# Nine unread products instead of sixteen ahead of unit 0's transposes, and alpha transposed behind group 0: a fused attention and MLP kernel on one Trainium2 core

## The chip, the cores and the metric

The kernel runs on one core of one Trainium2 chip. The metric is the device time in microseconds (us) of one execution. The engines of the core are PE (TensorE, matrix products), DVE (VectorE), ACT (ScalarE), POOL (GpSimd) and SP (SyncE, which here only issues transfers). A transfer (DMA) runs on 16 DMA engines, whichever queue issued it.

## The reference

A causal linear attention with a decay per head feeds a two-layer MLP with a leaky activation. Cut to what matters (B = 4 batches, H = 8 heads, S = 768 positions, D = 64; the MLP is 512 to 2048 to 512 wide):

```python
for b in range(nb):                        # blocks of 64 positions
    intra = einsum('bhic,bhjc->bhij', qb, kb) * Dmask       # lam ** (i - j), lower half
    intra = einsum('bhij,bhjd->bhid', intra, vb)
    inter = einsum('bhid,bhde->bhie', qb * lam_pow, kv_state)
    out[:, :, sl] = intra + inter
    kv_state = lam_block * kv_state + einsum('bhsd,bhse->bhde', kb * rev_pow, vb)
x = out.transpose(0, 2, 1, 3).reshape(B * S, H * D)
h = x @ w_in
g = maximum(h, 0) + alpha * minimum(h, 0)
result = g @ w_out
```

## The kernel before

**Units and chunks.** The sequence is cut into three windows of 256 positions (two blocks of 128 each). A *unit* is one window of one batch and four of its heads (`hh`), 24 units in all; four units make a *chunk* `c` of two batches, 512 rows of the MLP. For a unit the kernel casts keys, queries and values to 16 bits (`cast`, L247), multiplies the keys by their decay (`key_decayed`, L260, tile `kdec`), transposes keys and queries on PE through a PSUM bank (`transposed`, L303, tile `tpx`, four products of 128x128, then a copy into `qkT`), and multiplies the transposed queries by their decay (`decayed`, L321, tile `qdT`).

**Groups.** `cluster(old, new)` (L336) puts the products of two units together on PE: for the old unit the products with the carried state (L351) and with the masked scores (L380), for the new one the scores (L368, banks `s0` and `s1`) and the new state products (L395). They share the bank `acc`. Behind it stand the mask multiplication (DVE, L406), the copy of the finished attention output to `xT` (L234), and the state updates (ACT L426 and L427, DVE L430). What this text calls group 0 is `cluster(None, 0)`, group 1 is `cluster(0, 1)`.

**MLP.** `up(c, f)` (L449) multiplies `xT` by one 128-wide slice of `w_in` and applies the activation on ACT (L462) and DVE (L471, which needs `oma` = 1 - alpha); `down` (L478) multiplies by `w_out` and stores.

**Constants and the first microseconds.** `lam` and `alpha` come by two ACT-issued transfers (L61, L64). DVE zeroes the state tiles `RD` (`zero_states`, L115), POOL builds the identity `ident`. PE transposes a tile of `lam` (L170, `lam_ps`); its logarithm starts everything that decays. `slopes()` (L221) transposes alpha on PE (`at_ps`, L223) and has DVE make `oma` (L224).

**Unread products.** `fill(n, bank)` (L130) issues n products of 128x512 of the identity with itself (L134, tile `unread`), whose results nobody reads. They occupy PE in between. A bank has one tile (`op`, `tk`) or two in turn (`h`); whoever allocates a bank waits until its last tile has been read.

**What sets the order.** Nothing is reordered: each engine does its instructions in the order in which the program lists them, and waits on semaphores. Up to chunk 1 the order is a hand-written list (L554 to L771); from chunk 2 on, `weave` (L543) mixes attention steps and MLP steps. SP issues all loads of keys, queries and values in list order. `gate(i, which)` (L109) is a tiny transfer on SP that reads a slice of a weight, so that the loads behind it on SP wait until that slice has landed; POOL issues the loads of the weight slices (`load_win`, L95; `load_wout`, L101) in its own order between its casts. The start of the list around the change:

```python
    mask_logs(1)
    mask_logs(2)
    slopes()
    decay_mask(1)
...
    cast(0, "k16", "V")
    fill(16, "h")
    transposed(0, 1, "V", "tk")
    cast(1, "k16", "A")
    fill(3, "h")
    transposed(1, 1, "V", "h")
    load(0, 0, "q", 1)
    cast(1, "q16", "A")
    transposed(0, 0, "V", "op")
```

Of the kernel before, what the change touches and what calls it, by code (L numbers as in the profile page):

```python
# [11 lines left out]
def kernel(  # L12
# [16 lines left out]
    nc = tc.nc  # L29
# [42 lines left out]
    RD = {  # L72
        (b, hh): const.tile([128, 2, 2, 2, D], fp16, name=f"RD{b}_{hh}")
        for b in range(B)
        for hh in range(2)
    }
# [18 lines left out]
    def load_win(i):  # L95
        nc.gpsimd.dma_start(
            out=w_in_sb[:, :, ts(i, 512)],
            in_=moe_w_in[:, ts(i, 512)].rearrange("(g p) f -> p g f", p=128),
        )
# [14 lines left out]

    def zero_states(batches):  # L115
        for b in batches:
            for hh in range(2):
                nc.vector.memset(RD[b, hh], 0.0)

    zero_states((0, 1))  # L120
    ident = const.tile([128, 128], fp16, name="ident")
    make_identity(nc, ident)
    ident32 = const.tile([NF, NF], fp32, name="ident32")
# [2 lines left out]
    def bank_of(bank, name, dtype=fp32):  # L126
        pool = h_ps_pool if bank == "h" else ps
        return pool.tile([128, CH], dtype, tag=bank, name=name)

    def fill(n, bank="h"):  # L130

        t = bank_of(bank, "unread").rearrange("p (a j) -> p a j", a=4)
        for _ in range(n):
            nc.tensor.matmul(  # L134
                t, lhsT=ident, rhs=ident.unsqueeze(1).to_broadcast([128, 4, 128]), start=True, stop=True
            )

    lam_ps = h_ps_pool.tile([128, CH], fp32, tag="h", name="lam_ps")
    fill(2)

# [40 lines left out]
    def mask_logs(hp):  # L183

        for hl in range(2):
            h = 2 * hp + hl
            nc.vector.scalar_tensor_tensor(
                out=dmask[:, hl, hp],
                in0=rel_f,
                scalar=loglam[:, h : h + 1],  # L190
                in1=drop,
                op0=ALU.mult,
                op1=ALU.add,
            )

    def decay_mask(hp):
        nc.scalar.activation(dmask[:, :, hp], dmask[:, :, hp], AF.Exp)
# [23 lines left out]
    def slopes():  # L221
        at = h_ps_pool.tile([128, CH], fp32, tag="h", name="at_ps")
        nc.tensor.transpose(at[:, 0:NF], alpha_sb, ident32)  # L223
        nc.vector.tensor_scalar(  # L224
            out=oma, in0=at[:, 0:NF], scalar1=-1.0, scalar2=1.0, op0=ALU.mult, op1=ALU.add
        )
# [5 lines left out]
    def copy_on(eng, out, in_):  # L232
        if eng == "A":
            nc.scalar.activation(out, in_, AF.Copy)  # L234
        elif eng == "V":
            nc.vector.tensor_copy(out=out, in_=in_)
        else:
            nc.gpsimd.tensor_copy(out=out, in_=in_)  # L238
# [8 lines left out]
    def cast(n, name, eng):  # L247
        t = T.setdefault(n, {})
        if name == "v16":
            t[name] = half_pool.tile([128, 2, 4, D], fp16, tag=name, name=name)  # L250
            copy_on(eng, t[name], raw_of(n)[name])
            return
        if "qk16" not in t:
            t["qk16"] = half_pool.tile([128, 2, 2, 4, D], fp16, tag="qk16", name="qk16")
        copy_on(eng, t["qk16"][:, int(name == "k16")], raw_of(n)[name])
# [47 lines left out]
    def transposed(n, x, eng, bank):  # L303

        c, bi, hh = units[n]
        t = T.setdefault(n, {})
        if "qkT" not in t:
            t["qkT"] = qkt_pool.tile([128, 2, 2, 2, L], fp16, tag="qkT", name="qkT")
        tp = bank_of(bank, "tpx", fp16).rearrange("p (e h j) -> p e h j", e=2, h=2)
        for e in range(2):  # L310
            for hp in range(2):
                nc.tensor.transpose(  # L312
                    tp[:, e, hp, :],
                    t["qk16"][:, x, e, ds(2 * hp, 2)].rearrange("p l d -> p (l d)"),
                    ident,
                )
        copy_on(eng, t["qkT"][:, x], tp)
        if x == 0:
            t["qps"] = tp
# [233 lines left out]

    mask_logs(1)  # L554
    mask_logs(2)
    slopes()
    decay_mask(1)
    mask_logs(0)
    load(0, 0, "k", 0)
# [11 lines left out]
    cast(0, "v16", "A")  # L571
    decay_mask(3)
    cast(0, "k16", "V")
    fill(16, "h")
    transposed(0, 1, "V", "tk")
    cast(1, "k16", "A")
    fill(3, "h")
    transposed(1, 1, "V", "h")
    load(0, 0, "q", 1)
    cast(1, "q16", "A")  # L580
# [10 lines left out]
    decay_mask(0)  # L591
    fill(3, "tk")
    cluster(None, 0)
    transposed(1, 0, "V", "h")
    load_win(0)
    cast(2, "q16", "A")
    fill(5, "h")
    transposed(2, 0, "V", "op")
    load(0, 1, "q", 1)
    cast(2, "k16", "A")  # L600
# [33 lines left out]
    up(0, 5, 0, "h")  # L634
    up(0, 5, 1, "op")
    zero_states((2, 3))
    up(0, 3, None, "tk")
    up(0, 0, 1, "h")
# [175 lines left out]
```

## Time and profile before

| what | value |
|---|---|
| time, median of 3 runs (lowest to highest) | 221.18 us (220.04 to 221.42) |
| the profiled execution, its own time | 221.5 us |
| its span, first to last instruction | 219.5 us |
| mean granted PE clock | 1.000 |
| bytes moved by transfers | 33.90 MB, mean 154 GB/s |

The profile is of one execution. Its page gives busy times by engine, the span in forty slices of 5.49 us, the transfers, the chain of work that ended last, and the costliest groups; the trace behind it gives single instructions. Times in it count from the start of the span. The 2.0 us between the execution's time and its span lie outside the span.

### The profile page before, as it was taken

How to read it: one execution, taken by the hardware profiler on the slowest of the kernel's cores; microseconds unless marked ns; L12 is line 12 of the kernel's file. 1: busy time of each engine (PE TensorE's matmuls, PEld its weight loads, DVE VectorE, ACT ScalarE, POOL GpSimd, SP SyncE). 2: the span in 40 equal slices, each digit the busy share in tenths (PEclk: the TensorE clock that was granted, in tenths of full speed). 3: DMA queues.
4: the chain of work that ended last, by engine and by line, in shares of the span. 5: the costliest groups of instructions: out<-in, count | busy, mean ns of one | idle time of the engine just before them, and what ended most of it. 6: DMA issues, size and time to landing. Idle time of an engine off the chain costs nothing.

```text
span 219.5 us, 5216 instructions
## 1 busy us (share of the span) xinstructions
PE 209.1 (95%) x2079; PEld 106.9 (49%) x2079; DVE 131.8 (60%) x263; ACT 115.4 (53%) x223; POOL 89.6 (41%) x161
## 2 busy tenths in 40 slices
PE   4998899999996999999999999999999999999994
PEld 1455545554453544555545545544545444444453
DVE  7399788965696974866856555646546444444000
ACT  6747678955762565365465446445444434444121
POOL 3553056802577583597693583485331000000000
PEclk9999999999999999999999999999999999999999
DMA  6999997999989999689757877341211011100212
GB/s 168 296 235 169 245 262 193 190 197 302 238 249 122 314 284 178 185 222 218 191 118 198 217 177 196 82 99 49 51 48 48 3 48 49 48 39 12 96 48 96
DMA packets 62335, 33.90 MB, mean 154 GB/s; under 512 B 18135, under 2 KB 59367, under 8 KB 62311
## 3 DMA queue, kind: packets, MB, share of 16 engines
q1 hardware_dynamic: 58038, 29.37, 52.8%
q0 software_dynamic: 4224, 4.19, 12.1%
q8 instruction: 16, 0.26, 0.5%
q14 instruction: 9, 0.07, 0.1%
q10 hardware_dynamic: 48, 0.01, 0.0%
HBM read 27.27 MB, written 6.29 MB: 153 GB/s over the span
## 4 chain that ended last, share of the span: by engine, by line
PE 88%; ACT 4%; DMA 4%; DVE 2%; issue 1%; ACTq 0%; DVEq 0%
PE h_ps L454 37%; PE o_ps L484 30%; PE o_ps L507 6%; PE unread L134 4%; PE s L368 3%; DMA qkT<-qk 3%; PE acc L380 2%; PE acc L351 2%; PE acc L395 1%; PE tpx L312 1%; DMA alpha_sb<-in_moe_alpha_dram 1%; ACT xT L234 1%; ACT m L462 1%; ACT RD L426 1%; DVE R L430 1%
## 5 line engine op out<-in xcount | busy, mean ns | idle before, releaser
L471 DVE SCALAR_TENSOR_TENSOR g<-m,oma,h_ps 128x512 f16<-128x512 f32 (+1 forms) x100 | 71.5, 724 | 60.5 <-ACT m L462 59.5
L454 PE MATMUL h_ps<-xT,w_in_sb 128*128 128x512 f16 (+1 forms) x400 | 95.7, 371 | 0.3 <-ACT qkT L234 0.3
L462 ACT ACTIVATE m<-h_ps 128x512 f32<-128x512 f32 (+1 forms) x100 | 57.5, 580 | 63.2 <-PE h_ps L454 61.6
L484 PE MATMUL o_ps<-w_out_sb,g 128*128 128x512 f16 x320 | 81.1, 379 | 0.0
L454 PEld LDWEIGHTS <-w_in_sb 128*128 128x128 f16 x400 | 38.1, 98 | 42.1 <-issue 0.9
L484 PEld LDWEIGHTS <-g 128*128 128x128 f16 x320 | 30.3, 98 | 35.2
L444 POOL COPY RD<-R 64x128 f16<-64x128 f16 x64 | 18.5, 288 | 37.4 <-DVE R L430 35.5
L406 DVE TENSOR_TENSOR sm<-s,dmask 128x512 f16<-128x512 f32 x48 | 30.8, 683 | 3.7 <-PE s L368 3.4
L326 POOL TENSOR_TENSOR qdT<-qkT,qdecay 128x512 f16<-128x512 f16 (+1 forms) x20 | 21.4, 1071 | 11.4 <-DMA qkT<-qk 4.8
L264 POOL TENSOR_TENSOR kdec<-kraw,kdecay 128x512 f16<-128x512 f32 x21 | 21.9, 1046 | 5.1 <-DMA kraw<-in_k_dram 5.0
L497 ACT ACTIVATE o_sb<-o_ps 128x512 f32<-128x512 f32 (+1 forms) x25 | 14.5, 580 | 17.4 <-PE o_ps L507 11.1
L234 ACT ACTIVATE xT<-acc 128x512 f16<-128x512 f32 x21 | 12.5, 597 | 14.6 <-PE acc L395 11.9
L238 POOL CAST qk<-kraw 128x512 f16<-128x512 f32 x17 | 10.5, 618 | 21.7 <-DMA kraw<-in_k_dram 10.8
L430 DVE SCALAR_TENSOR_TENSOR R<-R,rdecay,acc 128x64 f16<-128x64 f16 x64 | 14.2, 274 | 1.7 <-ACT R L427 1.7
L134 PE MATMUL unread<-ident 128*128 128x512 f16 x45 | 13.8, 444 | 1.4 <-POOL ident masks.py:199 1.4
L507 PE MATMUL o_ps<-w_out_sb,g 128*128 128x512 f16 (+1 forms) x80 | 14.0, 337 | 0.0
L368 PE MATMUL s<-qkT 64*64 64x128 f16 x384 | 10.0, 222 | 1.7 <-DMA qkT<-qk 1.7
L234 ACT ACTIVATE qk<-qraw 128x512 f16<-128x512 f32 x18 | 11.2, 623 | 0.3 <-DMA qraw<-in_q_dram 0.3
L507 PEld LDWEIGHTS <-g 128*128 128x128 f16 x80 | 7.8, 98 | 6.2
L351 PEld LDWEIGHTS <-RD 128*128 128x128 f16 x80 | 6.1, 98 | 7.9 <-ACT m L462 1.1
L351 PE MATMUL acc<-qdT,RD 128*128 128x128 f16 x80 | 8.5, 219 | 1.4 <-ACT m L462 0.6
L238 POOL CAST v<-vraw 128x512 f16<-128x512 f32 x15 | 9.1, 608 | 1.6 <-PE h_ps L454 1.6
(54 smaller groups left out, 108.5 us busy)
## 6 DMA issues: line engine op xcount, KB each, us to landing
out_dram<-o_sb SPq DMA_DIRECT2D x23, 256.0 KB, 2.0
kraw<-in_k_dram SPq DMA_DIRECT2D x10, 512.0 KB, 5.5
qraw<-in_q_dram SPq DMA_DIRECT2D x10, 512.0 KB, 5.7
vraw<-in_v_dram SPq DMA_DIRECT2D x10, 512.0 KB, 5.7
w_in_sb<-in_moe_w_in_dram POOLq DMA_DIRECT2D x4, 512.0 KB, 7.7
w_out_sb<-in_moe_w_out_dram POOLq DMA_DIRECT2D x4, 512.0 KB, 7.2
kraw<-in_k_dram SPq DMA_DIRECT2D x4, 256.0 KB, 5.2
qraw<-in_q_dram SPq DMA_DIRECT2D x4, 256.0 KB, 5.3
```

The source lines that it names most:

```text
L134: nc.tensor.matmul(t, lhsT=ident, rhs=ident.unsqueeze(1).to_broadcast([128, 4, 128]), start=True, stop=True)
L234: nc.scalar.activation(out, in_, AF.Copy)
L238: nc.gpsimd.tensor_copy(out=out, in_=in_)
L264: engine(eng).tensor_tensor(out=kdec, in0=kr, in1=kdecay[:, ds(4 * hh, 4), :].rearrange("p h e -> p e h").unsqueeze(3).to_broadcast([128, ...
L326: engine(eng).tensor_tensor(out=qdT[:, :, :, p], in0=(t["qps"] if eng == "P" else t["qkT"][:, 0])[:, :, :, p], in1=qdecay[:, hh, :, :, p], ...
L351: nc.tensor.matmul(ot[a][:, hp, :].rearrange("p (e j) -> p e j", e=2), lhsT=RD[bb, ho][:, a, hp].rearrange("p h d -> p (h d)"), rhs=to["qd ...
L406: nc.vector.tensor_tensor(out=sm, in0=s[hl], in1=mask_of(hl, hh), op=ALU.mult)
L454: nc.tensor.matmul(h_ps[:, 0:n] if bi is None else h_ps[:, 0:n].rearrange("p (e j) -> p e j", e=2), lhsT=w_in_sb[:, gi, ts(f, 128)], rhs=x ...
L462: nc.scalar.activation(m[:, 0:n], h_ps[:, 0:n], AF.Relu, scale=-1.0)
L471: nc.vector.scalar_tensor_tensor(out=g, in0=mv, scalar=oma[:, f : f + 1], in1=hv, op0=ALU.mult, op1=ALU.add)
L484: nc.tensor.matmul(o_ps, lhsT=lhs(c, f, t), rhs=w_out_sb[:, f, :], start=(f == 0), stop=(f == NF - 1),)
L507: nc.tensor.matmul(o_ps[:, 0:n], lhsT=lhs(c, f, t), rhs=w_out_sb[:, f, ts(x, n)], start=(f == 0), stop=(f == NF - 1),)
```

## The change

Four things are edited. The two unread products ahead of the transpose of `lam` become four, and they read the zeroed state tile `RD[1, 1]` in place of the identity; that tile is now zeroed first. `slopes()` moves from the mask logarithms to the place behind group 0. Sixteen unread products ahead of unit 0's key transposes become nine. The three behind those transposes and the five behind unit 1's query transposes take the bank `tk` and not `h`. In all PE issues five products fewer; DVE does `oma` behind the state update of group 0, and `zero_states` counts down where it counted up. ACT, POOL and SP keep their instructions and their order.

```diff
     def zero_states(batches):
         for b in batches:
-            for hh in range(2):
+            for hh in (1, 0):
                 nc.vector.memset(RD[b, hh], 0.0)
 
-    zero_states((0, 1))
+    zero_states((1, 0))
...
-    def fill(n, bank="h"):
-
-        t = bank_of(bank, "unread").rearrange("p (a j) -> p a j", a=4)
+    def fill(n, bank="h", zeros=None):
+
+        t = bank_of(bank, "unread")
         for _ in range(n):
+            if zeros is not None:
+                nc.tensor.matmul(t, lhsT=zeros[:, 0:128], rhs=zeros, start=True, stop=True)
+                continue
             nc.tensor.matmul(
-                t, lhsT=ident, rhs=ident.unsqueeze(1).to_broadcast([128, 4, 128]), start=True, stop=True
+                t.rearrange("p (a j) -> p a j", a=4),
+                lhsT=ident,
+                rhs=ident.unsqueeze(1).to_broadcast([128, 4, 128]),
+                start=True,
+                stop=True,
             )
 
     lam_ps = h_ps_pool.tile([128, CH], fp32, tag="h", name="lam_ps")
-    fill(2)
+    fill(4, "h", RD[1, 1].rearrange("p a e h d -> p (a e h d)"))
...
     mask_logs(1)
     mask_logs(2)
-    slopes()
     decay_mask(1)
...
     cast(0, "k16", "V")
-    fill(16, "h")
+    fill(9, "h")
     transposed(0, 1, "V", "tk")
     cast(1, "k16", "A")
-    fill(3, "h")
+    fill(3, "tk")
     transposed(1, 1, "V", "h")
...
     fill(3, "tk")
     cluster(None, 0)
+    slopes()
     transposed(1, 0, "V", "h")
     load_win(0)
     cast(2, "q16", "A")
-    fill(5, "h")
+    fill(5, "tk")
     transposed(2, 0, "V", "op")
```

## The prediction

> **What bounds the kernel now.** I read the page first: span, engine shares, the forty slices of the DMA engines, the costliest group.
>
> ```profile
> span 219.5 us, 5216 instructions
> PE 209.1 (95%) x2079; PEld 106.9 (49%) x2079; DVE 131.8 (60%) x263; ACT 115.4 (53%) x223; POOL 89.6 (41%) x161
> DMA  6999997999989999689757877341211011100212
> L454 PE MATMUL h_ps<-xT,w_in_sb 128*128 128x512 f16 (+1 forms) x400 | 95.7, 371 | 0.3 <-ACT qkT L234 0.3
> ```
>
> PE is busy 95% of the span, and the 400 up-projection products waited 0.3 us in all (last column). From the first of them on, PE is an almost gapless queue in a written order: work that reaches it earlier ends the kernel earlier, one for one, unless a transfer takes the lead back. The DMA engines are nearly full for the first 16 slices, so that can happen. The change lies in the first two slices. There the chain of waits (start, length, what) reads:
>
> ```profile
> 4.14 0.26 PE at_ps L223
> 4.40 5.60 PE unread L134 x16
> 10.00 0.22 PE tpx L312 x4
> 10.22 0.65 PE unread L134 x3
> ```
>
> Alpha's transpose, which waited for alpha's load, starts at 4.14, and behind it stand sixteen unread products whose results nobody reads. They hold back unit 0's key transposes, although the timeline (start, length, engine, line; in brackets the idle time before and what ended it) shows the keys cast long before, and DVE idle 3.09 us for them:
>
> ```profile
> 6.75 0.42 DVE L236 CAST qk<-kraw 128x512 f16<-128x512 f32 x1
> 9.83 0.39 PE L312 MATMUL tpx<-ident,qk 128*128 128x128 f16 x4
> 10.26 0.42 DVE L236 COPY qkT<-tpx 128x512 f16<-128x512 f16 x1 [3.09 <-PE tpx L312]
> 7.65 0.61 ACT L234 ACTIVATE qk<-kraw 128x512 f16<-128x512 f32 x1
> 10.70 0.61 PE L312 MATMUL tpx<-ident,qk 128*128 128x128 f16 x8
> 11.94 0.42 PE L368 MATMUL s<-qkT 64*64 64x128 f16 x16
> 4.33 3.17 PE L134 MATMUL unread<-ident 128*128 128x512 f16 x7
> ```
>
> The last row gives PE's first pace: seven products in 3.17 us, the last one lasting about 0.61, so six steps of 0.427 us. The chain's three products from 10.22 take 0.65, or 0.217 each. The sixteen of the chain took 5.60, that is ten at the first pace and six at the second: PE halves its step near 8.6 us, though the granted clock of a window quoted below (third number from the end) reads 1.00. Both paces are used below.
>
> **The change part by part.** *Zeros.* The four products on zeros need only the first memset, not ident. The four memsets begin at 0.86 and take 1.09, so the first ends near 1.15; four steps of 0.427 end at 2.9. The lambda transpose behind them started at 2.85, so it moves by at most 0.1, and what follows it on ACT and DVE too. Their cover is the wait for lambda; without it they would cost 1.7. Against that 0.1, DVE no longer has oma between the mask logarithms, where it takes about 0.1 of its queue:
>
> ```profile
> 0.86 1.09 DVE L118 MEMSET RD<- 128x256 uint32 x4 [0.86 <-PEq L798]
> 2.85 0.27 PE L170 MATMUL lam_ps<-ident,lamc 8*128 8x8 f32 x1 [0.45 <-DVE lamc L163]
> 5.03 0.16 DVE L224 TENSOR_SCALAR oma<-at_ps 128x16 f32<-128x16 f32 x1
> ```
>
> So the key cast still ends at 6.75 + 0.42 = 7.17.
>
> *Nine for sixteen, alpha away.* PE goes on at about 3.2 without alpha. Nine products end at 3.2 + 9 x 0.427 = 7.04 even if all go at the slow pace. The key transposes then wait for the cast alone and start at 7.2 instead of 9.83: 2.6 us ahead.
>
> *The next three products move to bank tk.* That bank holds the key transposes until DVE has copied them, so here is a new wait. By the rows above the copy starts 0.43 after the transposes and takes 0.42: 7.63 to 8.05. The three products run from 8.08 and take 0.65, and the eight transposes behind them start at 8.73 instead of 10.70. Unit 1's keys, cast by ACT at 7.65 + 0.61 = 8.26, are there. The wait takes 0.6 of the 2.6; 1.97 is left. Copies follow at 9.16 to 9.92 and the scores of group 0 at 9.97 instead of 11.94.
>
> *What else group 0 needs.* These rows decide whether the lead goes on:
>
> ```profile
> 7.73 2.06 POOL L264 TENSOR_TENSOR kdec<-kraw,kdecay 128x512 f16<-128x512 f32 x2 [5.01 <-DMA kraw<-in_k_dram]
> 9.73 0.61 POOL L238 CAST v<-vraw 128x512 f16<-128x512 f32 x1
> 11.98 1.06 POOL L264 TENSOR_TENSOR kdec<-kraw,kdecay 128x512 f16<-128x512 f32 x1
> 11.99 1.34 DVE L326 TENSOR_TENSOR qdT<-qkT,qdecay 128x256 f16<-128x256 f16 x1
> 45.14 0.42 DVE L326 TENSOR_TENSOR qdT<-qkT,qdecay 128x256 f16<-128x256 f16 x1
> 13.32 0.62 ACT L234 ACTIVATE qk<-qraw 128x512 f16<-128x512 f32 x1
> 14.00 0.40 PE L312 MATMUL tpx<-ident,qk 128*128 128x128 f16 x4
> 5.89 0.69 SPq L87 DMA_DIRECT2D qraw<-in_q_dram  x1
> qraw<-in_q_dram SPq DMA_DIRECT2D x1, 256.0 KB, 5.3
> ```
>
> POOL's decayed keys depend on a load and stay put; unit 0's end at 7.73 + 2.06 = 9.79, and its state products want them at 12.16 - 1.97 = 10.19, so 0.4 of slack is left of 2.4. DVE's qdT took 1.34 instead of 0.42 because it stood beside a POOL tensor operation (11.98 to 13.04) and ended 0.29 after it. In the new order it falls at 9.95, beside POOL's cast that ends at 10.34, and ends near 10.63: that is 2.7 earlier than 13.33, so DVE does not lose the lead. The Trainium skill ("SBUF — State Buffer", Who interferes with whom) calls the port pair of VectorE and GpSimd an exclusive lock: the loser waits for the winner's whole instruction. The two qdT rows agree, and by that rule the delay would be the same 0.3 to 0.4.
>
> *Alpha behind group 0.* Its transpose is 0.26 by the chain's row, and oma 0.16 on DVE; nobody needs oma before the first up-projection, so it costs PE some 0.2. The transposes of unit 1's queries start near 10.65, five products on tk (which waits for no reader) fill to 11.95, and unit 2's query transposes need ACT's cast, which was the 13.32 row: 13.32 + 0.62 - 1.97 = 11.97. Its data came at 5.89 + 5.3 = 11.2 (the last two rows are that load's issue and its time to landing), just ahead of 11.35, so 0.15 of slack. They start at 12.0 instead of 14.00: 2.0. Group 1's scores stood on a DVE copy, and DVE is 2.3 to 2.7 ahead, so PE leaves group 1 with a lead of 2.0 to 2.3.
>
> *Where the lead meets loads.* The first up-projection stood at 22.32 and needs the first w_in slice, which landed at 10.28 + 6.7 = 17.0: it can come at 20. The next loads hang on a gate, a small transfer that waits for the second w_in slice. I hold that slice where it was: POOL issues the first pair from 10.28 on, behind work that does not move.
>
> ```profile
> 10.28 1.69 POOL L96 DMA_DIRECT2D w_in_sb<-in_moe_w_in_dram  x2
> w_in_sb<-in_moe_w_in_dram POOLq DMA_DIRECT2D x1, 512.0 KB, 6.7
> 22.32 1.05 PE L454 MATMUL h_ps<-xT,w_in_sb 128*128 128x256 f16 x8
> 29.21 0.61 POOL L238 CAST qk<-kraw 128x512 f16<-128x512 f32 x1 [10.84 <-DMA kraw<-in_k_dram]
> 32.16 0.39 PE L312 MATMUL tpx<-ident,qk 128*128 128x128 f16 x4
> 30.95 0.61 POOL L238 CAST qk<-qraw 128x512 f16<-128x512 f32 x1
> 33.80 0.72 PE L312 MATMUL tpx<-ident,qk 128*128 128x128 f16 x8 [0.28 <-DVE g L471]
> 22.60 3.75 SPq L87 DMA_DIRECT2D vraw<-in_v_dram  x1
> vraw<-in_v_dram SPq DMA_DIRECT2D x1, 512.0 KB, 10.1
> 34.77 0.62 ACT L234 ACTIVATE v<-vraw 128x512 f16<-128x512 f32 x1
> ```
>
> Unit 4's keys are cast at 29.82 at the earliest and PE wanted them at 32.16: room for 2.3. Its queries are cast at 31.56, wanted at 33.80: room for 2.2. Its values land at 22.60 + 10.1 = 32.7 and were cast at 34.77: room for 2.1. These three cap the lead at about 2.1. Later transfers are released by POOL's w_out issues, which follow PE, so they move with it; the page's seventh DMA slice (32.9 to 38.4) stands at 7 tenths, room for those slices to start earlier.
>
> The sum: 2.63 (transposes), minus 0.66 (tk wait and order), plus 0 to 0.3 (DVE), capped at 2.1. I take 2.1. The profiled execution took 221.5 us, 0.3 above the median of 221.18; 221.5 - 2.1 = 219.4. Ends of the unknown prices: a gate that opens 1 us later leaves a lead of 1.1; one that opens some 0.6 earlier, because the microsecond in which the DMA engines were busy only 0.67 (the row below, next to last number) is filled, lifts the cap to 2.7.
>
> ```profile
> 18.00:19.00 1.00, 1.00 (x36) 0.67 (x34) 1.00 (x3) 0.99 (x3) 0.37 (x1) 1.00 0.67 82
> ```
>
> **The rivals.** *A: the transfers keep the lead.* The engines are full, the gated loads stay where they are or come later because the second pair of w_in slices is now issued 2.3 earlier among them. For it: the three rooms above are all near 2.1, so every microsecond that a load slips is lost at once. Against it: those slices stand behind the first pair on one queue. With slips of 1 to 2 the lead is 0 to 1.1 and the time 220.4 to 221.5.
>
> *B: PE falls to its slow pace* (the slower side). With seven unread products fewer, PE idles up to 1.1 us ahead of 7.2 (if its pace doubles at 5, nine products end near 6.1) and again 0.5 behind the key transposes. If that keeps or brings back the 0.427 step, every microsecond of fast work costs another. It decides where 2.1 us of such work has run slow, that is if the slow pace lasts to about 12.3; if it lasts to 16.7, the loss is 2.1 more, and the time 223.6. Against it: PE once stood still 1.68 us, and the eight products behind it kept the short step ((1.90 - 0.38) / 7 = 0.217, the last lasting 0.38):
>
> ```profile
> 69.83 0.42 PE L368 MATMUL s<-qkT 64*64 64x128 f16 x16 [1.68 <-DMA qkT<-qk]
> 70.53 1.90 PE L454 MATMUL h_ps<-xT,w_in_sb 128*128 128x512 f16 x8
> ```
>
> The Trainium skill ("TensorE: Matmul & The Clock Gate", Part 1 and Part 4) states that the array runs at half rate until a free-running window of some 3.4 us was busy, falls back after an idle one, and that transposes do not count as busy. By that rule the idle here would not be long enough for a fall, while a window of mostly transposes and waits could be. The two rows agree on the first half; no row here shows the second.
>
> *C: more than forecast.* The gated loads come earlier as above: lead 2.3 to 2.7, time 218.8 to 219.2.
>
> **How the numbers follow.** Forecast (218.9 to 220.0): 0.52. A: 0.24. B: 0.09, most of it between no change and 223.6. C: 0.15. The range for 8 in 10 runs from C's lower part to the top of A: 218.4 to 221.5. About 1%, or 2.2 us, is what a measurement of this kernel can tell from no change. Against 221.18 that is 218.97, just under my 219.4: all but a little of C (0.13) and some two fifths of the forecast's own band (0.22) would count as faster, 0.35; slower is the far part of B, 0.05; the rest, 0.60, is the same.
>
> **What would show it.** The key transposes start at 7.2, right behind DVE's cast; the eight that follow at 8.7, after a wait of PE for the copy on tk; group 0's scores at 10.0; the first up-projection near 20.1; unit 4's transposes at 29.9 and 31.6. If the first holds and the last two stay at 32 to 34, A is right; steps of 0.427 behind 9 us show B; scores later than 10.5 mean a wait that I have not priced.

## The result and the profile after

The median fell from 221.18 us to 219.92 us (17 runs each, 220.04 to 222.53 and 218.70 to 222.11). The ratio is 0.9943, with a 95% interval of 0.9921 to 0.9964: 1.26 us faster. The interval excludes no change, though the gain is less than the 1% that the prediction took as the least that can be told from none. The forecast was 219.4 us, a lead of 2.1 us against the profiled execution that it started from. The direction, the range and the place in the kernel were right; two fifths of the forecast lead did not come.

The page of the profile after, its span, PE's share and the group of the up-projections:

```profile
span 218.7 us, 5205 instructions
PE 208.0 (95%) x2074; PEld 106.4 (49%) x2074; DVE 131.4 (60%) x263; ACT 115.3 (53%) x223; POOL 89.6 (41%) x161
L461 PE MATMUL h_ps<-xT,w_in_sb 128*128 128x512 f16 (+1 forms) x400 | 95.7, 371 | 0.3 <-ACT qkT L241 0.3
```

PE is as full as before and does the same 95.7 us of up-projections; its busy time is 1.1 us shorter, with five products fewer. The kernel is still one PE queue, 0.8 us shorter in this pair of profiles (219.5 and 218.7; the profiled execution after took 220.56 us, against 221.5 before).

The timeline of PE after, over the front of the kernel (start, length, what; in brackets PE's idle time before and what ended it):

```profile
1.19 1.89 PE L135 MATMUL unread<-RD 128*128 128x512 f16 x4 [1.19 <-DVE RD L118]
3.01 0.27 PE L177 MATMUL lam_ps<-ident,lamc 8*128 8x8 f32 x1
3.21 3.43 PE L137 MATMUL unread<-ident 128*128 128x512 f16 x9
7.30 0.40 PE L319 MATMUL tpx<-ident,qk 128*128 128x128 f16 x4 [0.66 <-DVE qk L243]
8.21 0.81 PE L137 MATMUL unread<-ident 128*128 128x512 f16 x3 [0.52 <-DVE qkT L243]
8.86 0.61 PE L319 MATMUL tpx<-ident,qk 128*128 128x128 f16 x8
10.09 0.42 PE L375 MATMUL s<-qkT 64*64 64x128 f16 x16
13.28 0.42 PE L375 MATMUL s<-qkT 64*64 64x128 f16 x16
20.29 1.05 PE L461 MATMUL h_ps<-xT,w_in_sb 128*128 128x256 f16 x8
```

The steps that the prediction named stand where it put them (its figure in brackets): key transposes 7.30 (7.2), the eight behind them 8.86 (8.7), scores of group 0 at 10.09 (10.0), first up-projection 20.29 (20.1, before 22.32). The bracket at 7.30 says that the keys' cast on DVE ends the wait, no longer the unread products; the one at 8.21 is the new wait for bank `tk`. The lead at the first up-projection is 2.03 us. The timeline after, where unit 4 needs its transfers:

```profile
19.47 0.74 SPq L113 DMA_DIRECT2D gates<-w_in_sb  x1
26.87 0.61 POOL L245 CAST qk<-kraw 128x512 f16<-128x512 f32 x1 [10.53 <-DMA kraw<-in_k_dram]
30.13 0.39 PE L319 MATMUL tpx<-ident,qk 128*128 128x128 f16 x4
31.77 0.72 PE L319 MATMUL tpx<-ident,qk 128*128 128x128 f16 x8 [0.28 <-DVE g L478]
```

Here the forecast had its cap. It did not bind: in this pair unit 4's keys are cast 2.3 us earlier than before (29.21), PE arrives 2.03 earlier (32.16 and 33.80 before), and the transposes do not wait for a load. The lead is lost later, in chunk 2. The first score groups of that chunk, before and then after:

```profile
59.28 0.42 PE L368 MATMUL s<-qkT 64*64 64x128 f16 x16
64.40 0.42 PE L368 MATMUL s<-qkT 64*64 64x128 f16 x16
```

```profile
57.25 0.42 PE L375 MATMUL s<-qkT 64*64 64x128 f16 x16
62.65 0.28 PE L358 MATMUL acc<-qdT,RD 128*128 128x128 f16 x2 [0.32 <-POOL RD L451]
63.35 0.42 PE L375 MATMUL s<-qkT 64*64 64x128 f16 x16 [0.42 <-DMA qkT<-qk]
68.98 0.42 PE L375 MATMUL s<-qkT 64*64 64x128 f16 x16 [1.83 <-DMA qkT<-qk]
```

At 57.25 the lead is still 2.03. At 63.35 it is 1.05. Of this loss 0.42 is a wait of PE for the DMA transpose of unit 10, and 0.32 a wait for a state tile that POOL copies (`RD`); the kernel before had neither. At 68.98, unit 11's scores (before 69.83, with a wait of 1.68), it is 0.85, and so it stays to the end.

### The profile page after: what moved, and what is told of

Read it like the earlier page. It is cut to its first block, busy times and chain, and to the rows that moved or that the text cites. A ratio compares the mean times of both kernels' runs of the same rounds, so it can differ in the third digit from the quotient of the medians.

```text
span 218.7 us, 5205 instructions
## 1 busy us (share of the span) xinstructions
PE 208.0 (95%) x2074; PEld 106.4 (49%) x2074; DVE 131.4 (60%) x263; ACT 115.3 (53%) x223; POOL 89.6 (41%) x161
## 3 DMA queue, kind: packets, MB, share of 16 engines
q0 software_dynamic: 4224, 4.19, 11.9%
## 4 chain that ended last, share of the span: by engine, by line
PE 87%; ACT 4%; DVE 4%; DMA 3%; issue 1%; SPq 0%; ACTq 0%
PE h_ps L461 37%; PE o_ps L491 30%; PE o_ps L514 6%; PE s L375 3%; DMA qkT<-qk 3%; PE acc L387 2%; PE acc L358 2%; PE tpx L319 2%; PE acc L402 1%; DVE dmask L194 1%; PE unread L137 1%; ACT m L469 1%; PE unread L135 1%; ACT xT L241 1%; ACT RD L433 1%
## 5 line engine op out<-in xcount | busy, mean ns | idle before, releaser
L461 PE MATMUL h_ps<-xT,w_in_sb 128*128 128x512 f16 (+1 forms) x400 | 95.7, 371 | 0.3 <-ACT qkT L241 0.3
L137 PE MATMUL unread<-ident 128*128 128x512 f16 x36 | 10.6, 423 | 0.5 <-DVE qkT L243 0.5
```

What stands on the lines that cost most here:

```text
L461: nc.tensor.matmul(h_ps[:, 0:n] if bi is None else h_ps[:, 0:n].rearrange("p (e j) -> p e j", e=2), lhsT=w_in_sb[:, gi, ts(f, 128)], rhs=x ...
```

## The experiments

Two theories followed from this pair. Theory 1: the front gives 2 us, and chunk 2 takes a part of it back, since the query load of units 10 and 11 is issued by SP behind unit 8's DMA transpose and lands too late for a PE that is early. Theory 2, its rival: the pair is not typical, the front gives less than 2 us in most executions, and chunk 2 costs nothing new. In what follows "front" is the start of the first up-projection, and "rest" is the span minus that. The medians of the kernel before in the three sets were 221.34, 221.30 and 221.42 us.

**1. The loads of units 10 and 11 ahead of unit 8's transpose, after and before.** The same edit on both kernels:

```
+    load(2, 1, "q", None)
+    load(2, 1, "v", None)
     transposes(8, "D", False)
...
     key_decayed(11, "G")
-    load(2, 1, "q", None)
-    load(2, 1, "v", None)
```

> The changed kernel, with the loads of unit 10's and 11's queries and values (batch 1 of chunk 2) issued on SP ahead of unit 8's transpose instead of behind it. Theory 1: PE's lead of 2.0 us is whole until 62 us, and 1.2 of it is lost there because that load stands on SP behind a transpose that waits for a cast. Then unit 10's query cast follows POOL's decayed keys near 58.2 (59.6 in the changed kernel), PE no longer waits for unit 10's transpose at 63, and the end comes 1.0 to 1.2 us earlier than in the changed kernel: ratio to before 0.989 to 0.990. Theory 2, the lead is lost to the DMA engines themselves, which are full: the transposes land as late as now and the ratio stays at 0.994.

> The kernel before, with only the same two loads issued ahead of unit 8's transpose. Theory 1: in the kernel before PE is 2.0 us later, reaches unit 10's scores just as its transpose lands, and has no lead to lose, so the ratio is 0.998 to 1.001. Theory 3, the place of the loads costs time whatever PE's lead is: the gain is the same 1 us as on the changed kernel, ratio 0.995.

Measured: 1.0012 (0.9984 to 1.0040) on the kernel after and 1.0102 (1.0074 to 1.0130) on the one before. The remedy cost about as much in both, 0.7% and 1.0% against the unedited kernels. The timeline of the edited kernel after shows why, in SP's queue and on PE:

```profile
54.48 6.36 SPq L289 DMA_TRANSPOSE qkT<-qk  x2
60.63 0.64 PE L375 MATMUL s<-qkT 64*64 64x128 f16 x16 [3.21 <-DMA qkT<-qk]
```

Unit 8's transpose, now issued at 54.48 behind two loads, released PE only at 60.63, after 3.21 us of waiting (3.31 in the edited kernel before). In the kernel after, it was issued at 52.63 and the group stood at 57.25 without a wait. The wait also cost more than itself. The page of the edited kernel after has the granted clock of forty slices, and the twelfth, from 60.7 us, stands at 0.7; below it are the sixteen up-projection products behind the group, in this kernel and then in the kernel after:

```profile
PEclk9999999999979999999999999999999999999999
61.42 4.78 PE L461 MATMUL h_ps<-xT,w_in_sb 128*128 128x512 f16 x16
```

```profile
57.73 3.63 PE L461 MATMUL h_ps<-xT,w_in_sb 128*128 128x512 f16 x16
```

From 60.6 to 63.5 the granted clock was 0.50, and the products took 1.15 us longer. In the edited kernel before it was 0.50 from 62.9 to 66.1, and the same products took 5.31. The eight executions of the edited kernel after with a mean clock of 0.992 or less took 222.07 us or more, the four with 1.000 at most 220.99. So the order of that queue matters, but none of the expected ratios came true: PE no longer waited for units 10 and 11, the edit had moved the wait to unit 8, where it also slowed PE, and so it tells nothing on how much the first wait costs.

**2. Sixteen unread products again, the rest as after.**

```
-    fill(9, "h")
+    fill(16, "h")
```

> The changed kernel with sixteen unread products again in front of unit 0's key transposes, all else as changed. From 3.2 us on, with the pace doubling at 6.0 as in the changed kernel's trace, sixteen end at 8.1, so the key transposes start at 8.1 instead of 7.3 and the lead at group 0 is 1.2 instead of 2.0. Theory 1, a lead over 0.85 is lost at 62 us anyway: the ratio to before stays at 0.994 to 0.995, and PE does not wait at 63. Rival, every microsecond at the front is worth its share at the end: ratio 0.997 to 0.998. If nine instead of sixteen were the whole gain, the ratio would be 1.000.

Measured: 0.9960 (0.9934 to 0.9987), between the two expectations. The front stood at 20.80, half a microsecond behind the kernel after. PE was free for the key transposes at 8.05 instead of 7.30, yet most of the gain remained: with PE busy from 1.19 on and no wait for alpha, sixteen products end well ahead of the 9.83 of the profile before.

**3. Alpha's transpose back in the front, nine products as after.**

```
     mask_logs(2)
+    slopes()
...
     cluster(None, 0)
-    slopes()
```

> The changed kernel with alpha's transpose back among the mask logarithms, in front of the nine products. PE then waits for alpha until 4.1, nine products at the slow pace end near 8.2, the key transposes start near 8.2 and the lead at group 0 is 1.1. Theory 1: ratio to before 0.994 to 0.995. Rival, every microsecond at the front is worth its share at the end: 0.997 to 0.998.

Measured: 0.9953 (0.9928 to 0.9978), front 20.47. PE waited 0.83 for alpha's load and the key transposes started at 7.66. Its profile is the shortest of all, 216.8 us, and PE waited little in chunk 2. The timeline of its second and third score group there:

```profile
62.55 0.42 PE L375 MATMUL s<-qkT 64*64 64x128 f16 x16
67.16 0.42 PE L375 MATMUL s<-qkT 64*64 64x128 f16 x16 [0.83 <-DMA qkT<-qk]
```

Against the profile before this is a lead of 1.85 at the front and at 62.55 alike, with no wait. With the program of chunk 2 unaltered, the loss that theory 1 took as given is absent here: it is not there in every execution.

**4. Units 9 and 10 exchanged in chunk 2 (order 8, 9, 11, 10), after and before.** The second group, then unit 9's, takes its queries from the load that unit 8 already had. The edit exchanges the two numbers in `key_decayed`, the casts of queries and values, `transposes`, `decayed` and `cluster`:

```
-    cast(10, "q16", "G")
-    transposes(10, "D", False)
+    cast(9, "q16", "G")
+    transposes(9, "D", False)
...
-    cluster(8, 10, "V")
+    cluster(8, 9, "V")
```

> The changed kernel with units 9 and 10 exchanged in the order of chunk 2 (8, 9, 11, 10 instead of 8, 10, 11, 9) from the decayed keys on, so that the unit behind 8 needs the queries that landed at 52 and not those that land at 59.6. Theory 1, the lead is lost to the late load of unit 10's queries: the second transpose of the chunk is issued near 58.8 instead of 60.3, PE does not wait at 63, and the end is 0.8 to 1.2 us earlier than in the changed kernel, ratio to before 0.988 to 0.991. Theory 2, the loss is in the DMA engines, where the transposes stand behind the loads: it lands near 62.3 anyway and the ratio is 0.993 to 0.995.

> The kernel before with the same exchange of units 9 and 10. Theory 1: PE comes 2.0 us later there and hardly waits for the second transpose, so the exchange gains at most 0.4 us: ratio 0.998 to 1.001, and the changed kernel with it is 1.8 to 2.0 us faster than this one. Rival, the exchange helps whatever the lead is: as much as on the changed kernel.

Measured: 0.9903 (0.9867 to 0.9938), 219.28 us, on the kernel after, the best version of all; 0.9988 (0.9956 to 1.0019) on the kernel before. In the first, the second group stood at 62.18 without a wait. The medians of the two edited kernels lie 1.77 us apart, more than the 1.26 of the unedited ones. That agrees with theory 1, but the interval overlaps that of the kernel after (0.9921 to 0.9964), so the exchange is not proved to be worth anything.

**5. Unit 9's query cast and transposes ahead of unit 10's decay, after and before.**

```
+    cast(9, "q16", "G")
+    transposes(9, "D", False)
     decayed(10, "G")
     cast(10, "v16", "A")
-    cast(9, "q16", "G")
-    transposes(9, "D", False)
     cluster(8, 10, "V")
```

> The changed kernel with unit 9's query cast and its transpose put ahead of unit 10's qdT on POOL (by one instruction), because that qdT waits for PE. The last transpose of the chunk is then released by the transpose of unit 11 in front of it on SP, near 64.6 instead of 65.6; PE's wait of 1.8 us at 67 falls to about 0.8. If that wait takes part of the lead: ratio to before 0.989 to 0.991. If the transpose lands as late as before because the DMA engines or the transpose in front of it set the time: 0.994.

> The kernel before with the same move of unit 9's query cast. Its wait at 68 was 1.7 us and would fall to 0.7: ratio 0.995 to 0.996 if POOL's order set it, 1.000 if the DMA engines did. The difference to the changed kernel with the same move tells what the lead is worth when that wait is short: 2.0 us by the theory that the lead is lost in this place, 1.3 if it is not.

Measured: 0.9937 (0.9912 to 0.9961) and 1.0018 (0.9989 to 1.0047): no difference to either unedited kernel. PE still waited 1.43 and 1.03 us at the third group. That group reads unit 11's transpose, and the edit moves unit 9's, which stands behind it on SP, so it could not shorten this wait directly. The edited kernel before also waited 0.81 at the second group, unit 10's, although its front was late (21.30).

The four profiles with the front of before (the kernel before and its three edits, which all lie behind 50 us) now speak on theory 2. In the timelines of the edits of 1, 4 and 5 in turn, the sixteen unread products and the first up-projection:

```profile
4.29 5.54 PE L134 MATMUL unread<-ident 128*128 128x512 f16 x16
21.73 1.05 PE L454 MATMUL h_ps<-xT,w_in_sb 128*128 128x256 f16 x8
```

```profile
4.28 5.32 PE L134 MATMUL unread<-ident 128*128 128x512 f16 x16
21.49 1.05 PE L454 MATMUL h_ps<-xT,w_in_sb 128*128 128x256 f16 x8
```

```profile
4.29 5.11 PE L134 MATMUL unread<-ident 128*128 128x512 f16 x16
21.30 1.05 PE L454 MATMUL h_ps<-xT,w_in_sb 128*128 128x256 f16 x8
```

The profile before, on which the forecast rests, has 5.66 and 22.32: the latest of the four. How long the sixteen products take depends on how long PE stays at its first pace. With fifteen steps of 0.427 or 0.217 us and a last product of 0.38, the lengths 5.66, 5.54, 5.32 and 5.11 mean 9.6, 9.1, 8.0 and 7.0 slow steps, so the pace doubled at 8.5, 8.2, 7.7 and 7.3 us. The four fronts average 21.71. The four profiles with the front of after (the kernel after and its edits of 1, 4 and 5) stand at 20.29, 20.38, 20.03 and 20.49, on average 20.30; there the key transposes start at 7.30 in each, whatever the pace was. So the front is worth 1.41 us on average, as far as four profiles of each can tell, not 2.03.

**6. All nine unread products away.**

```
-    fill(9, "h")
```

> The changed kernel without the nine unread products: PE stands still from the lambda transpose at 3.3 to the key cast at 7.25. The products are there to double PE's pace, which in the traces so far came at 6.0 with them (four zeros and nine) and at 7.3 to 8.5 in the kernel before. If the pace needs PE busy (theory), it is still 0.427 us a step at 8.2, the three and three products in front of group 0 take 1.3 each and not 0.65, group 0's scores start at 11.4 to 12.0 instead of 10.09 and the ratio to before is 0.999 to 1.003. If the pace comes with time alone (rival), the scores start at 10.1 and the ratio is 0.994.

Measured: 1.0006 (0.9983 to 1.0029), so the whole gain is gone. Its timeline of PE, and below it the row of the windows view for 7.3 to 11.9 us (third number from the end: granted clock):

```profile
7.30 0.61 PE L319 MATMUL tpx<-ident,qk 128*128 128x128 f16 x4 [4.02 <-DVE qk L243]
8.42 1.44 PE L137 MATMUL unread<-ident 128*128 128x512 f16 x3 [0.52 <-DVE qkT L243]
22.04 1.05 PE L461 MATMUL h_ps<-xT,w_in_sb 128*128 128x256 f16 x8
```

```profile
7.30:11.90 4.60, 4.08 (x18) 1.99 (x18) 1.70 (x4) 2.17 (x6) 4.35 (x6) 1.00 1.17 291
```

The key transposes start at the same 7.30, but PE has been idle for 4.02 us and goes on at the slow pace: four transposes take 0.61 instead of 0.40, three unread products 1.44 instead of 0.81. It lasts to about 12 us, and costs 1.74 us at the first up-projection (22.04 against the average of 20.30). This is rival B's mechanism, in a kernel that leaves the nine products out. The granted clock reads 1.00 through this slow stretch, unlike the 0.50 behind the wait in experiment 1, so the column does not show every slow stretch.

**7. Two products of the identity instead of four on zeros.**

```
-    fill(4, "h", RD[1, 1].rearrange("p a e h d -> p (a e h d)"))
+    fill(2)
```

> The changed kernel with the two products on the identity of before in the place of the four on zeros. If the zeros count as work for PE's pace, as the change at 6.0 in the changed kernel against 7.3 to 8.5 before suggests, the pace now doubles later than 7.3, and the products between unit 0's transposes and group 0 may still run slow: scores at 10.1 to 10.8, ratio 0.994 to 0.998. If only products on other data count, nothing moves: scores at 10.0 and 0.994.

Measured: 0.9962 (0.9934 to 0.9990), front 20.25, pace doubled near 6.2 us. The front is that of the kernel after within its spread, and so is the time at which the pace doubled; the interval leaves open a loss of some tenths of a per cent.

**8. The three products behind unit 0's key transposes back on bank `h`, without the wait for `tk`.**

```
     cast(1, "k16", "A")
-    fill(3, "tk")
+    fill(3, "h")
```

> The changed kernel with the three products behind unit 0's key transposes on bank h again, where they wait for no copy. PE's wait of 0.52 us at 8.2 goes, the eight transposes start near 8.2 instead of 8.86 and group 0's scores near 9.5 instead of 10.09. Theory: DVE's qdT, now at 9.6, stands beside POOL's cast and transfer issue and ends no earlier than before, near 11.2, so group 1's scores stay at 13.0 to 13.3 and the ratio at 0.993 to 0.995. Rival, the wait on tk is a price of the change that comes back in full: 0.991 to 0.992.

Measured: 0.9937 (0.9910 to 0.9964). The wait is gone and the timeline is earlier by what it was priced at:

```profile
8.18 0.61 PE L319 MATMUL tpx<-ident,qk 128*128 128x128 f16 x8
9.41 0.42 PE L375 MATMUL s<-qkT 64*64 64x128 f16 x16
19.84 1.05 PE L461 MATMUL h_ps<-xT,w_in_sb 128*128 128x256 f16 x8
```

The eight transposes come 0.68 earlier, the front 0.45; the end does not follow by an amount that can be measured. DVE's `qdT` stood ahead of POOL's transfer issue and took 0.43, so group 1's scores came at 12.56, not at the expected 13.0 to 13.3. The nine products took 2.82 us here, which puts the doubling near 4.6, some 1.5 us behind the four products on zeros. In the profiles without products on zeros the pace doubled only after some 3 us of unbroken work or more (4.3 to 7.3 at the least). This speaks for products on zeros counting as work; it is one profile.

**9. The exchange of 4, and unit 0's decayed queries read from PSUM.**

```
-    decayed(0, "V")
+    decayed(0, "P")
```

> The changed kernel with units 9 and 10 exchanged (as in f1) and unit 0's qdT computed from the PSUM bank of the transposes instead of from the copy in SBUF, so that DVE reads one operand only from SBUF. In five of the six profiles with the changed front qdT took 0.85 to 1.28 us beside POOL's transfer issue, in f1 0.42. If two SBUF operands are what makes it wait, it takes about 0.45 every time, group 0's mask products start at 10.6 and group 1's scores at 13.0; the ratio is 0.988 to 0.990. If it waits all the same: 1.1 us, 13.3, and 0.990 to 0.992.

Measured: 0.9918 (0.9886 to 0.9949), front 20.04. The timelines of DVE's `qdT` beside POOL's issue of the two `w_in` loads, after and then in this kernel:

```profile
9.65 1.68 POOL L96 DMA_DIRECT2D w_in_sb<-in_moe_w_in_dram  x2
10.15 1.08 DVE L333 TENSOR_TENSOR qdT<-qkT,qdecay 128x256 f16<-128x256 f16 x1
```

```profile
9.89 1.69 POOL L96 DMA_DIRECT2D w_in_sb<-in_moe_w_in_dram  x2
9.96 0.41 DVE L333 TENSOR_TENSOR qdT<-tpx,qdecay 128x256 f16<-128x256 f16 x1
```

In the kernel after, the multiplication lasts until just before POOL's issue ends (11.23 and 11.33); here it took 0.41. But it started 0.07 behind the start of the issue, and the exchange alone, with both operands in SBUF, took 0.42 where it started 0.04 behind (10.14 and 10.10). So the run does not tell the operand from the time of the start. Group 1's scores start at 13.03, as they did with the exchange alone (13.02; 13.28 in the kernel after). By the median this adds nothing to the exchange.

## Why the prediction came out as it did

**Right: the mechanism of the front.** The cast on DVE became what the key transposes wait for, the wait on `tk` cost 0.52 to 0.68 (priced 0.6), and the lead went through both groups. The zeros moved the lambda transpose by 0.16 (3.01 against 2.85; priced at most 0.1), and the key cast by 0.08.

**Mis-sized: "start at 7.2 instead of 9.83: 2.6 us ahead".** The 7.2 held in every profile with that front. The 9.83 is one draw from 9.83, 9.67, 9.44 and 9.24, whose mean is 9.55, and it is the latest, so the term measured 2.25 on average. The Trainium skill ("TensorE: Matmul & The Clock Gate", Part 1) says that the window which decides the pace is free-running, so that its change falls differently in each run; the spread of 7.3 to 8.5 agrees, and with that sentence the 9.83 should have been taken as a draw. The forecast did set its profiled execution 0.3 above the median, but a difference of 0.3 in the total hid 0.6 in the front.

**Wrong in place: DVE "ends near 10.63".** `qdT` was put beside POOL's cast of the values. In the profile after, POOL's first load had landed earlier, the decayed keys began at 7.09 instead of 7.73, and the neighbour was the issue of the `w_in` loads; `qdT` ended at 11.23. The profile before, in turn, held the only long `qdT` (1.34) among the four with that front; the other three show 0.42 or 0.43. So the prediction expected a shorter `qdT` from the new order, and on average it was longer. Group 0 to group 1 takes 3.20 us on average over the four profiles after (13.28, 13.37, 13.02, 13.47), and 3.04 over the four before (15.30, 14.71, 14.47, 14.29). The average leads in order: 2.25 at the transposes, 1.56 at the scores of group 0, 1.41 at the first up-projection, 1.26 at the end. The Trainium skill ("SBUF — State Buffer", Who interferes with whom) has DVE's two-input multiplication block against POOL's reads, and infers that it does not meet descriptor generation. Here `qdT` lasted 0.85 to 1.28 us beside the issue in six profiles, which does not agree, and the measurement decides; no run took the issue away, so that the issue is the cause is not shown.

**Wrong: the cap of 2.1 from unit 4's rooms.** In the pair the gate opened 1.3 us earlier:

```profile
20.77 0.74 SPq L113 DMA_DIRECT2D gates<-w_in_sb  x1
```

But 20.77 was a late draw too. In the other three profiles with the front of before it stood at 19.76, 19.55 and 19.48, in the four with the front of after at 19.47 to 19.57, and in the run without the nine products, whose front is late, at 19.39. So the gate hardly follows the front, and the rooms were not 2.3 and 2.2 for unit 4's keys and queries but 3.0 to 3.7 in those other three profiles. The cap was read from that one of the four profiles in which it was tightest. The earlier loads are what rival C needs, but the front gave no longer lead for them to let through. Rival A did not occur at the place that the text names; a loss of its kind sits at 63 and 69 us.

**The loss in chunk 2.** The view of PE's waits gives the sum over all groups, how often PE waited, and the longest; here for the kernel after, sixteen products, alpha in front, no nine, no zeros, and no `tk` wait, in that order:

```profile
PE s L375 <- DMA qkT<-qk: 2.2, 2, 1.8
```

```profile
PE s L375 <- DMA qkT<-qk: 1.3, 2, 1.1
```

```profile
PE s L375 <- DMA qkT<-qk: 0.8, 1, 0.8
```

```profile
PE s L375 <- DMA qkT<-qk: 1.2, 2, 0.8
```

```profile
PE s L375 <- DMA qkT<-qk: 1.9, 2, 1.5
```

```profile
PE s L375 <- DMA qkT<-qk: 2.1, 3, 1.5
```

All six have the unaltered chunk 2, as has the kernel before with 1.68.

| kernel | front | rest | wait in chunk 2 | rest without it | ratio to before |
|---|---|---|---|---|---|
| before | 22.32 | 197.2 | 1.7 | 195.5 | 1 |
| no nine | 22.04 | 196.8 | 1.2 | 195.6 | 1.0006 |
| sixteen | 20.80 | 196.9 | 1.3 | 195.6 | 0.9960 |
| alpha in front | 20.47 | 196.3 | 0.8 | 195.5 | 0.9953 |
| after | 20.29 | 198.4 | 2.2 | 196.2 | 0.9943 |
| no zeros | 20.25 | 197.9 | 1.9 | 195.9 | 0.9962 |
| no `tk` wait | 19.84 | 198.1 | 2.1 | 195.9 | 0.9937 |

The last column but one is taken from unrounded times. The rests differ by 2.1 us, and without this wait by 0.7: what an execution loses behind the front, it loses mostly there. The three earliest fronts have the three largest waits, which is what theory 1 says. They alone also wait for POOL's state tile at 62 us (0.3, 0.3 and 0.2 in the last three rows); without that too, the rests lie between 195.5 and 195.8. But these are seven single executions, the kernel before has 1.7 at the latest front, the kernel without the nine waits 0.37 at unit 10's group with a front of 22.04, and the exchange that should mend it is not told from the kernel after by its interval. So theory 2 carries the larger part of the miss, as far as four profiles of each front can tell: of the 0.84 us between 2.1 and 1.26, 0.69 lies in the front (2.1 against 1.41). The remaining 0.15 is less than the intervals resolve, and whether chunk 2 takes it, or takes more from fronts ahead of 20.4, stays open.

**The parts of the change.** No single part that was undone takes the whole gain away: undoing the count, alpha's place, the zeros or the `tk` bank leaves 0.9937 to 0.9962. What takes it away is PE standing still until the keys are cast (experiment 6).

## What to carry to other kernels

Size a gain from several profiles when the stage starts with PE's slow pace or with a load: the step that is removed may be a draw, and the one profile at hand its far end. Work that only keeps PE awake has a use up to the next real dependency: here nine products or sixteen differ by half a microsecond at the first up-projection, but none at all costs the whole gain; no run tried a number in between. An earlier front can be lost again to a transfer that does not move with it, so look for the waits behind it, and for what a long wait does to PE's pace, before moving it again.

## What the runs showed of the hardware

- PE's pace doubles at a time that differs between executions of the same front: 7.3 to 8.5 us with the front of before, about 4.6 to 7.2 with the four products on zeros or the nine behind them. After 4.02 us of idle time, it stayed slow until about 12 us, while the granted clock read 1.00 throughout.
- In the middle of the kernel, a wait of PE of 3.21 or 3.31 us was followed by about 3.4 us at a granted clock of 0.50 (an estimate from its mean in single microseconds: 0.69, 0.50, 0.50 and 0.60 from 60 on, 0.91, 0.50, 0.50, 0.50 and 0.88 from 62 on), and sixteen products took 4.78 or 5.31 us instead of 3.63. No clock below 1.00 followed the waits of up to 1.83 us in that chunk.
- PE idle for 0.4 to 1.3 us ahead of unit 0's key transposes did not bring the slow pace back in any profile.
- DVE's `qdT` with two SBUF operands took 0.85 to 1.28 us in the six profiles in which it started 0.2 to 0.7 us behind the start of POOL's issue of two loads, and ended 0.1 to 0.2 ahead of the issue's end. It took 0.42 where it started 0.04 behind that start (the exchange on the kernel after) or 1.21 behind it (no nine). An estimate from these: its end less 0.42 lies 1.1 to 1.2 us behind the issue's start in all six, so it seems to be held up to there.
- A DMA transpose that was issued on SP behind two loads landed 6.1 us later and released PE at 60.63 (issued at 54.48); issued ahead of them, at 52.63, it landed 3.6 us later.
